# Second-level Winograd sums made by adding DMAs, gated blocks added in the store path, and one more product split twice

## The chip, the cores and the metric

The kernel runs on one core of a Trainium2 chip. The metric is the device time of one execution in microseconds (us). Before the change three runs gave 1852.26, 1853.48 and 1853.75 us, so the median is 1853.48 us.

## What is computed

All in float32, with S = 2048 tokens, D = 1024 and F = 3584:

```python
x = A_x                                              # 1 x 2048 x 1024
g = sigmoid((x * gate_w).sum(-1, keepdims=True))
a = einsum("bsd,ed->bse", x, dft_hid_re)
b = einsum("bsd,ed->bse", x, dft_hid_im)
y = einsum("ts,bse->bte", dft_seq_re, a) - einsum("ts,bse->bte", dft_seq_im, b)
h = einsum("bsd,df->bsf", x, B_w1) + B_b1
h = where(h > 0, h, 0) ** 2
o = einsum("bsf,fd->bsd", h, B_w2) + B_b2
return g * y + (1 - g) * o
```

## The kernel before

Four matrix products do nearly all of the work, one after the other: stage x (the hidden DFT, whose result is called `ab`), stage C (the sequence DFT of `ab`, result `y`, which is multiplied by the gate and kept in DRAM as `gy`), stage h in two parts (`x` times `w1`, then ReLU and square, kept in DRAM as `h`; part 0 has four rows of tiles to a step, part 1 has three), and stage o (`w2` times `h`, then bias, `1 - g`, plus `gy`, then `out`).

Each stage is a Winograd form of Strassen's product: 2 x 2 blocks, seven products in place of eight, in the order 1, 2, 5, 6, 3, 7, 4 (`WIDE`, `TALL_C`, `TALL_O`). Left factors come from sums S1 to S4 of the left blocks, right factors from T1 to T4 of the right blocks (`FACTORS`). A product can be split a second time in the same way ("twice"): seven smaller products in place of eight steps of matmuls, with sums of its own (`SUMS_L2`, `SUMS_R2`). Which products are split twice stands in `TWICE_X`, `TWICE_C`, `TWICE_O`, `TWICE_H`; the numbers in `TWICE_C` and `TWICE_O` say for how many pairs of inner blocks. What isn't split twice runs through `direct`. Stages x and h use `wide`, stages C and o use `tall`.

The data are 128 x 1024 float32 tiles (512 KB). Every factor goes to TensorE as two parts: ScalarE copies the tile to a rounded `hi`, VectorE subtracts to get `lo`, and a tile product is three matmuls, hi*hi, hi*lo and lo*hi (`Operand`, `Group.run`). For 256-column left tiles both parts lie in one tile, `both`. So for each factor there is one pass of ScalarE and one of VectorE; each Winograd sum costs one more pass of VectorE. A finished group of matmuls lies in PSUM (four pools of two banks); ScalarE or VectorE takes it up (`put`, `add`), which frees the banks for a later group. Where a group goes on from an earlier result, ScalarE first copies that to PSUM (`Group.prepare`).

SBUF is cut into 55 slots of one tile (`SLOTS`). Loads are issued by SyncE's queue (SP). Stores, and all DMAs that add into their destination (`accum_op=ADD`), are issued by GpSimd's queue (POOL). Before the change two kinds of adding DMA are in use: with `lands`, a first-level sum of two blocks from DRAM is made by a plain load of one and an adding load of the other into the same slot (`Part.load`); and stage h stores T1 and T3 of `h` for stage o with a store and an adding store into a DRAM block (`Kept.store`, `sums_far`).

The kernel records all its instructions first. `plan` gives each a due time and runs a model of engines, queues and slots; `emit` writes the instructions out in the order that came of it and chains each engine to that order, so every instruction has line L1209 in the profile. Inside a queue nothing overtakes.

The second-level right sums before the change, all with subtraction:

```python
SUMS_R2 = {"T1": ((0, 1), (0, 0), SUB), "T2": ((1, 1), "T1", SUB), "T3": ((1, 1), (0, 1), SUB),
           "T4": ((1, 0), "T2", SUB)}
```

Their blocks are loaded whole into slots of their own, and VectorE makes each sum in a slot of its own. In part 1 of stage h, `TWICE_H[1]` is `(1, 2, 5, 3, 4)`: products 6 and 7 run through `direct`, at 8 steps of 18 matmuls (144) each, and a product split twice takes 7 steps (126). At the end of stage o, `final` multiplies each of the 15 first output blocks by its gate row, loads its `gy` block over SP and adds it with VectorE, then stores; the last block goes by halves (`last`).

Of the kernel before, what the change touches and what calls it, by code (L numbers as in the profile page):

```python
# [19 lines left out]
WIDE, TALL_C, TALL_O = ((1, 2, 5, 6, 3, 7, 4),) * 3  # L20
TWICE_X, TWICE_C, TWICE_O = (1, 2, 5, 3, 4), {1: 1, 2: 4, 3: 4, 4: 4, 5: 2}, {1: 2, 2: 3, 3: 3, 4: 3, 5: 2, 6: 1}
# [24 lines left out]
SUMS_L2 = {"S1": ((1, 0), (1, 1), ADD), "S2": ("S1", (0, 0), SUB), "S3": ((0, 0), (1, 0), SUB),  # L46
           "S4": ((0, 1), "S2", SUB)}
SUMS_R2 = {"T1": ((0, 1), (0, 0), SUB), "T2": ((1, 1), "T1", SUB), "T3": ((1, 1), (0, 1), SUB),
           "T4": ((1, 0), "T2", SUB)}
# [5 lines left out]
def gated_mix_kernel(ctx: ExitStack, tc: tile.TileContext, x4, xn, w4, ct, w1a, w1b, w2, b1, b2, gw, out):  # L55
# [53 lines left out]
    class Op:  # L109


        def __init__(self, engine, name, args, kwargs):
# [6 lines left out]
            if name == "dma_start":  # L119
                self.time, self.load = ISSUE[engine], n * P * 4 / RATE[0]  # L120
                if "accum_op" in kwargs:
                    self.time, self.load = ADDING[0], ADDING[1] * self.load
# [8 lines left out]
            self.after, self.then, self.new, self.latest, self.landed = set(), [], [], None, False  # L131

# [167 lines left out]

    class Operand:
# [107 lines left out]
    steps = []  # L409
# [8 lines left out]
    class Sums:  # L418


        def __init__(self, get, sums, keep=False, far=(), lands=(), shared=None, near=()):
# [30 lines left out]
        def early(self, key):  # L452

            e = self.of(key, near=True)
            self.made[key] = Part(e.far())
# [6 lines left out]
    def seven(order, second, new_u, c11, c12, c21, c22, put, add, direct, twice, slots, sign=1, flip=False):  # L462
# [12 lines left out]
        def six(k, ps):  # L475
            put(u, k, ps)
            add(c12, k, ps, 3 in before[6], c22, sign)
# [6 lines left out]
        for p in order:  # L484
            if p == 1:
                product(1, None, one, False, slots)
            elif p == 2:
                product(2, one, c11, True, slots, 6 in before[2])
            elif p == 3:
                product(3, c12, c12, True, 0, sign=sign)  # L490
# [4 lines left out]
            elif p == 6 and 6 in second:  # L495
                twice(6, one, u, lambda k: add(c12, k, u[k].slot, 3 in before[6], c22, sign), 2 in before[6], 1, -1)
# [11 lines left out]
    def tall(left, right, ksteps, order, second, first, target, final, last=None, lands={}, shared=None):  # L508
# [55 lines left out]
        def twice(p, old, new, ends, drop, sign, less=1):  # L564
# [25 lines left out]
            r2 = {q: Sums(lambda j, c, q=q: right[2 * q + j, c].of(r), SUMS_R2, True) for q in range(k)}  # L590
# [11 lines left out]
            def onward(dst, key, ps):  # L602

                if old:
# [3 lines left out]
                    if less < 0:  # L608
# [19 lines left out]
            def five(_, ps):  # L628
                key = block(1, 1)
                add(new, block(0, 1), ps)  # L630
                if old:
# [7 lines left out]
                    nc.vector.tensor_tensor(flat(at), flat(at), flat(tmp[0, 0].slot), op=ADD)  # L639
# [7 lines left out]
                else:  # L647
                    add({key: new[key]}, key, ps, ends and not more, src={key: new[block(1, 0)]})
# [45 lines left out]
    def wide(left, right, rows, order, second, target, final, sign=1, onto_old=False, flip=False, lands={},  # L694
             shared=None):
# [67 lines left out]
        def twice(p, old, new, ends, drop, sign, less=1):  # L763
# [3 lines left out]
            r2 = Sums(lambda q, c: right[q, c].of(r), SUMS_R2, True)  # L767

            def takes(first, m, c, ends=False):
                def f(rp, ps):  # L770
                    k = m, c, rp
                    if not first:
                        add(new, k, ps, ends, sign=sign)
# [19 lines left out]
            for p2, group in (*(begin if steps else begin[::-1]), (3, other), (6, chain), (2, last), (7, chain),  # L793
# [13 lines left out]
    def x_stage():  # L807
# [7 lines left out]
        def final(dst, ps, sign):  # L815
            if ps is not None:
# [5 lines left out]
             final, -1, True, lands=LAND_X, shared=shared)  # L822
# [3 lines left out]
    h_far = {(j, q, t): Kept(f"h{j}{q}{t}") for j in range(2) for q in range(7) for t in range(4) if j + t // 2}  # L826
    sums_far = {(q, c): {k: Kept(f"{k}{q}{c}", 2) for k in ("T1", "T3")} for q in range(7) for c in range(2)}

    def h_stage(part):
# [3 lines left out]
        def target(i, n, k):  # L833
# [4 lines left out]
            far = [h_far[i, q, 2 * n + c]] if i + n else []  # L838
# [412 lines left out]
```

## Time and profile before

| | |
|---|---|
| median of three runs | 1853.48 us |
| the profiled execution's own time | 1852.4 us |
| span in its trace (first to last instruction) | 1850.6 us |
| matmuls of 128 x 512 | 8034 |
| VectorE instructions | 1746 (16 of them read back an accumulator, and go with an instruction of the program), busy 1753.4 us |
| ScalarE instructions | 1254, busy 1090.8 us |
| DMAs issued by SP and POOL | 628 and 260 |

The profiled execution's time is 1.8 us above its span, and 1.1 us below the median. Times within the trace count from the start of the span. "PE" is TensorE, "PEld" its weight load, "DVE" VectorE, "ACT" ScalarE. A row of the view by stretches shows for each stretch its length, then each engine's busy time with its number of instructions, the granted clock, and the mean busy share of the core's DMA engines. A row of the timeline shows start, duration, engine, operation, and in brackets how long the engine had been idle and what ended that.

### The profile page before, as it was taken

The page shows a single profiled execution, that of the slowest core. Times are in us where ns is not written, and L with a number is a line of the kernel's source. Part 1 is how long each engine was busy: PE and PEld are TensorE (multiplying, and loading weights), DVE is VectorE, ACT ScalarE, POOL GpSimd, SP SyncE. Part 2 cuts the span into 40 slices and gives each one's busy share as a digit, 9 for nine tenths or more (in the row PEclk, how much of TensorE's full clock was granted, in tenths as well). Part 3 has the DMA queues.
Part 4 walks back from the last instruction along what each step waited for, and adds up shares of the span by engine and source line. Part 5 has one row for each costly group of instructions (what it writes and reads, how often), then busy time and mean ns, then how long its engine had stood idle before and what let it go on. Part 6 is the DMA issues. An engine that isn't in the chain of part 4 may idle for free.

```text
span 1850.6 us, 22073 instructions
## 1 busy us (share of the span) xinstructions
PE 1831.6 (99%) x8078; PEld 1511.9 (82%) x8078; DVE 1753.4 (95%) x1746; ACT 1090.8 (59%) x1254; POOL 169.2 (9%) x264
## 2 busy tenths in 40 slices
PE   9999999999999999999999999999999999999998
PEld 7888887888888888888888887888888888888886
DVE  8997999889999999899999999978999999999998
ACT  6474656364453454466583699777976554456352
POOL 0100200001110001000110112202210001100001
PEclk9999999999999999999999999999999999999999
DMA  7762989449998379544563798857994658838935
GB/s 236 261 243 87 377 305 394 167 151 292 294 371 348 136 248 393 210 149 171 165 244 103 243 310 268 264 187 222 310 339 175 216 178 288 301 131 314 362 121 204
DMA packets 131484, 452.37 MB, mean 244 GB/s; under 512 B 14496, under 2 KB 23984, under 8 KB 131376
## 3 DMA queue, kind: packets, MB, share of 16 engines
q1 hardware_dynamic: 94016, 323.15, 48.0%
q0 software_dynamic: 37072, 127.43, 22.5%
q8 instruction: 63, 1.03, 0.2%
q10 hardware_dynamic: 288, 0.39, 0.1%
q14 instruction: 45, 0.37, 0.1%
HBM read 341.85 MB, written 109.06 MB: 244 GB/s over the span
## 4 chain that ended last, share of the span: by engine, by line
PE 82%; DVE 7%; ACT 4%; issue 3%; DMA 3%; POOL 0%; SPq 0%; DVEq 0%; ACTq 0%; POOLq 0%
PE ps L1209 82%; DVE lo L1209 3%; ACT h L1209 2%; DMA raw<-in_x 2%; ACT hi L1209 2%; DVE h L1209 1%; DVE o L1209 1%; DVE sum L1209 1%; DMA raw<-in_ct 0%; DMA h<-h 0%; DVE u L1209 0%; DVE both L1209 0%; ACT ps L1209 0%; DVE raw L1209 0%; POOL h L1209 0%
## 5 line engine op out<-in xcount | busy, mean ns | idle before, releaser
L1209 PE MATMUL ps<-hi 128*128 128x512 f32 x1866 | 727.0, 390 | 8.6 <-ACT hi L1209 3.5
L1209 PE MATMUL ps<-hi,lo 128*128 128x512 f32 x1866 | 725.9, 389 | 0.6 <-DVE lo L1209 0.6
L1209 PE MATMUL ps<-lo,hi 128*128 128x512 f32 x1866 | 725.7, 389 | 0.4 <-DVE lo L1209 0.4
L1209 ACT ACTIVATE hi<-raw 128x1024 fp32r<-128x1024 f32 (+2 forms) x367 | 373.1, 1033 | 252.4 <-DVE raw L1209 119.8
L1209 PE MATMUL ps<-hi,both 128*128 128x512 f32 x1624 | 501.9, 389 | 1.1 <-DVE both L1209 1.1
L1209 DVE TENSOR_TENSOR lo<-raw,hi 128x1024 fp32r<-128x1024 f32 (+2 forms) x367 | 429.7, 1192 | 30.2 <-ACT hi L1209 19.5
L1209 PEld LDWEIGHTS ps<-hi 128*128 128x128 f32 x1866 | 350.6, 188 | 85.1 <-ACT hi L1209 7.3
L1209 PEld LDWEIGHTS ps<-hi,lo 128*128 128x128 f32 x1866 | 350.4, 188 | 74.3 <-DVE lo L1209 1.6
L1209 PEld LDWEIGHTS ps<-lo,hi 128*128 128x128 f32 x1866 | 350.3, 188 | 73.9 <-DVE lo L1209 1.3
L1209 ACT ACTIVATE hi<-sum 128x1024 fp32r<-128x1024 f32 x244 | 249.7, 1036 | 198.3 <-DVE sum L1209 140.2
L1209 PEld LDWEIGHTS ps<-hi,both 128*128 128x128 f32 x1624 | 304.7, 188 | 65.2 <-DVE both L1209 1.9
L1209 PE MATMUL ps<-lo,both 128*128 128x512 f32 x812 | 315.9, 389 | 0.0
L1209 DVE TENSOR_TENSOR lo<-sum,hi 128x1024 fp32r<-128x1024 f32 (+1 forms) x244 | 288.2, 1196 | 12.3 <-PE ps L1209 8.8
L1209 DVE TENSOR_TENSOR raw<-raw 128x1024 f32<-128x1024 f32 (+1 forms) x178 | 211.1, 1205 | 5.6 <-DMA raw<-in_x 1.8
L1209 DVE TENSOR_TENSOR sum<-raw 128x1024 f32<-128x1024 f32 (+2 forms) x180 | 184.3, 1031 | 9.7 <-PE ps L1209 5.8
L1209 PEld LDWEIGHTS ps<-lo,both 128*128 128x128 f32 x812 | 152.4, 188 | 31.6
L1209 DVE TENSOR_TENSOR sum<-raw,sum 128x1024 f32<-128x1024 f32 (+2 forms) x135 | 147.5, 1094 | 3.7 <-PE ps L1209 2.8
L1209 ACT ACTIVATE u<-ps 128x1024 f32<-128x1024 f32 x103 | 99.1, 968 | 84.6 <-PE ps L1209 68.5
L1209 ACT ACTIVATE both<-sum 128x512 fp32r<-128x512 f32 x116 | 70.9, 623 | 72.2 <-DVE sum L1209 57.8
L1209 DVE TENSOR_TENSOR h<-h,ps 128x1024 f32<-128x1024 f32 (+1 forms) x84 | 87.8, 1068 | 2.4 <-ACT u L1209 1.9
L1209 ACT ACTIVATE ps<-u 128x1024 f32<-128x1024 f32 x70 | 67.7, 970 | 25.2 <-DVE u L1209 13.6
L1209 ACT ACTIVATE both<-raw 128x512 fp32r<-128x512 f32 x87 | 53.8, 624 | 46.3 <-DVE raw L1209 21.2
(60 smaller groups left out, 915.5 us busy)
## 6 DMA issues: line engine op xcount, KB each, us to landing
raw<-in_ct SPq DMA_DIRECT2D x133, 512.0 KB, 8.3
raw<-in_w SPq DMA_DIRECT2D x92, 512.0 KB, 5.6
raw<-h SPq DMA_DIRECT2D x78, 512.0 KB, 5.4
raw<-ab SPq DMA_DIRECT2D x72, 512.0 KB, 9.9
raw<-copy SPq DMA_DIRECT2D x62, 512.0 KB, 4.7
raw<-in_x SPq DMA_DIRECT2D x59, 512.0 KB, 6.4
T<-h POOLq DMA_DIRECT2D x48, 512.0 KB, 10.0
copy<-raw POOLq DMA_DIRECT2D x46, 512.0 KB, 6.8
```

What stands on the lines that cost most here:

```text
L1209: made = getattr(real[op.engine], op.name)(*(actual(a) for a in op.args), **{k: actual(v) for k, v in op.kwargs.items()})
```

## The change

Six things change together.

1. The second level's signs are turned so that T1 to T4 are sums (`SUMS_R2` as in the first level; S1 and S4 of `SUMS_L2` and the take-up of product 5 change sign with them).
2. A second-level T1 or T3 whose blocks both come from DRAM can be made in place: the class `Onto` keeps one block's slot and issues an adding load of the other block into it. For that, the base block's own `hi` and `lo` have to be made before. `LAND2_C`, `LAND2_H` and `LAND2_O` say where this is done; stage x is left as it was. Where T1 is made so in `wide`, the second-level products begin with 1 instead of 5.
3. Stage h stores T1 and T3 for 7 of 14 right blocks only (`MADE`), and all blocks of `h`; stage o makes the other T1 and T3 with adding loads (`LAND_O`). In stage C, T3 of the first level no longer lands by an adding load (`LAND_C`).
4. For the first 12 output blocks, `gy` is added by an adding DMA from DRAM (`ADD_O`), ahead of the store on the same queue.
5. Product 6 of part 1 of stage h is split twice.
6. The planner counts adding stores to DRAM as dearer, holds back POOL DMAs due more than 20 us later while SP's or ScalarE's queue moves data, and a DMA held so gets a wait on the VectorE or ScalarE instruction that ended last in its model.

Counted in the two kernels' written-out instructions:

| | before | after |
|---|---|---|
| 128 x 512 matmuls | 8034 | 8016 |
| VectorE instructions: stages x, C, h part 0, h part 1, o | 215, 556, 232, 200, 527 | 215, 538, 220, 219, 510 |
| ScalarE instructions | 1254 | 1244 |
| DMAs by SP | 628 | 604 |
| DMAs by POOL | 260 | 306 |
| of these, adding into a slot | 38 | 108 |
| of these, adding into DRAM | 32 | 16 |

The diff, cut to its core:

```diff
-LAND_X, LAND_C, LAND_H, LAND_O = {"T1": 4, "T3": 2}, {"T1": 16, "T3": 4}, ({"T1": 4}, {"T1": 4, "T3": 4}), {}
+LAND_X, LAND_C, LAND_H, LAND_O = {"T1": 4, "T3": 2}, {"T1": 16}, ({"T1": 4}, {"T1": 4, "T3": 4}), {"T1": 14, "T3": 4}
-TWICE_H = (1, 2, 5, 3, 4, 6), (1, 2, 5, 3, 4)
+ADD_O = range(12)
+LAND2_X, LAND2_C, LAND2_H, LAND2_O = {}, {1: {"T1": 1, "T3": 1}, 2: {"T1": 4, "T3": 4}, 3: {"T1": 4, "T3": 4}, 4: {"T1": 2, "T3": 2}, 5: {"T1": 1, "T3": 1}}, ({1: ("T1", "T3"), 2: ("T1", "T3"), 5: ("T1", "T3"), 3: ("T1", "T3"), 4: ("T1", "T3"), 6: ("T1", "T3")}, {1: ("T3",), 2: ("T3",), 5: ("T1", "T3"), 3: ("T1", "T3"), 4: ("T1", "T3"), 6: ("T3",)}), {2: {"T1": 3, "T3": 3}, 3: {"T1": 2, "T3": 2}, 4: {"T1": 2, "T3": 2}, 5: {"T1": 1, "T3": 1}, 6: {"T1": 1, "T3": 1}}
+MADE = {"T1": 7, "T3": 7}
+TWICE_H = (1, 2, 5, 3, 4, 6), (1, 2, 5, 3, 4, 6)
...
-ADDING = 0.85, 2.1
+ADDING = 0.85, 2.1, 2.65
...
-LATE = 80.0
+LATE, PATIENT = 80.0, (20.0, 0)
...
-SUMS_R2 = {"T1": ((0, 1), (0, 0), SUB), "T2": ((1, 1), "T1", SUB), "T3": ((1, 1), (0, 1), SUB),
-           "T4": ((1, 0), "T2", SUB)}
+SUMS_R2 = {"T1": ((0, 1), (0, 0), ADD), "T2": ((1, 1), "T1", ADD), "T3": ((1, 1), (0, 1), ADD),
+           "T4": ((1, 0), "T2", ADD)}
...
+    class Onto(Near):
+        def __init__(self, base, b):
+            super().__init__("onto")
+            self.blocks, self.b = [base], b
+            base.uses += 1
...
+        def sum(self):
+            base, b = self.blocks[0], self.b
+            self.slot, self.done = base.slot, base.done
+            nc.gpsimd.dma_start(self.slot, b.at if isinstance(b, Kept) else b, accum_op=ADD)
...
                 a, b, op = self.sums[key]
+                other = self.get(*a if a != (1, 1) else b) if key in self.ontos else None
+                if key in self.ontos and not isinstance(other, (Near, View)) and not isinstance(
+                        self.get(*b if a != (1, 1) else a), (Near, View)):
+                    self.made[key] = Onto(self.of(b if a != (1, 1) else a), other)
+                    return self.made[key]
...
-            for p2, group in (*(begin if steps else begin[::-1]), (3, other), (6, chain), (2, last), (7, chain),
+            for p2, group in (*(begin if steps and "T1" not in r2.ontos else begin[::-1]), (3, other), (6, chain), (2, last), (7, chain),
                               (4, chain)):
...
-    h_far = {(j, q, t): Kept(f"h{j}{q}{t}") for j in range(2) for q in range(7) for t in range(4) if j + t // 2}
-    sums_far = {(q, c): {k: Kept(f"{k}{q}{c}", 2) for k in ("T1", "T3")} for q in range(7) for c in range(2)}
+    h_far = {(j, q, t): Kept(f"h{j}{q}{t}") for j in range(2) for q in range(7) for t in range(4)}
+    sums_far = {(q, c): {k: Kept(f"{k}{q}{c}", 2) for k in spread(MADE, 2 * q + c, 14)} for q in range(7)
+                for c in range(2)}
...
-            ready(add, cycle((nc.sync,)))
+            lands = len(made_o) in ADD_O
+            made_o.append(dst)
+            if not lands:
+                ready(add, cycle((nc.sync,)))
...
-            nc.vector.tensor_tensor(flat(dst.slot), flat(dst.slot), flat(add.slot), op=ADD)
+            if lands:
+                nc.gpsimd.dma_start(dst.slot, gy[i, n, c, rp].at, accum_op=ADD)
+            else:
+                nc.vector.tensor_tensor(flat(dst.slot), flat(dst.slot), flat(add.slot), op=ADD)
+                add.used()
...
+                    if (e == "gpsimd" and op.due - t > PATIENT[0] and len(free) >= PATIENT[1]
+                            and any(q in moving or rings[q] for q in ("sync", "scalar"))):
+                        op.held = True
+                        continue
+                    if op.held:
+                        op.gate = done[-1]
...
+        if op.gate:
+            tc.add_manual_dep(made.ins, op.gate.made, mybir.DependencyInfo(
+                mybir.DependencyClass.Sync, mybir.DependencyReason.DATA), reason="held")
```

More of the change, by code (lines that the diff above doesn't have):

```diff
@@ L121, in __init__ @@
                 if "accum_op" in kwargs:
-                    self.time, self.load = ADDING[0], ADDING[1] * self.load
+                    far = outs[0].base.home == "fixed"
+                    self.time, self.load = ADDING[0], ADDING[2 if far else 1] * self.load
             elif engine == "tensor":
@@ L454, in early @@
             e = self.of(key, near=True)
-            self.made[key] = Part(e.far())
+            self.made[key] = e.far()
             return e
@@ L476, in six, with five @@
             put(u, k, ps)
-            add(c12, k, ps, 3 in before[6], c22, sign)
+            if 5 in before[6]:
+                add(c12, k, ps, 3 in before[6], c22, sign)
+        def five(k, ps):
+            put(c22, k, ps)
+            add(c12, k, ps, True)
         def seven(k, ps):
@@ L488, in seven @@
                 product(2, one, c11, True, slots, 6 in before[2])
+            elif p == 3 and 5 in before[3]:
+                product(3, c12, c12, True, 0, sign=sign)
             elif p == 3:
-                product(3, c12, c12, True, 0, sign=sign)
+                assert 6 in before[3] and sign == 1
+                product(3, u, c12, False, slots)
+            elif p == 5 and 3 in before[5] and 5 in second:
+                twice(5, None, c22, lambda k: add(c12, k, c22[k].slot, True), False, 1)
+            elif p == 5 and 3 in before[5]:
+                direct(5, None, slots, five, [c22, c12], 1)
             elif p == 4 and 7 in before[4]:
@@ L495, in seven @@
             elif p == 6 and 6 in second:
-                twice(6, one, u, lambda k: add(c12, k, u[k].slot, 3 in before[6], c22, sign), 2 in before[6], 1, -1)
+                twice(6, one, u, (lambda k: add(c12, k, u[k].slot, False, c22, sign)) if 5 in before[6] else False,
+                      2 in before[6], 1, -1)
             elif p == 7 and 7 in second:
@@ L629, in five @@
                 key = block(1, 1)
-                add(new, block(0, 1), ps)
+                add(new, block(0, 1), ps, less=1 if old else -1)
                 if old:
@@ L647, in five @@
                 else:
-                    add({key: new[key]}, key, ps, ends and not more, src={key: new[block(1, 0)]})
+                    add({key: new[key]}, key, ps, ends and not more, src={key: new[block(1, 0)]}, less=-1)
             fresh = old is not new
@@ L772, in f @@
                     if not first:
-                        add(new, k, ps, ends, sign=sign)
+                        add(new, k, ps, ends, sign=-sign if c else sign)
                     elif old:
@@ L1134, in finish @@
         op.landed = True
+        if op.engine in ("vector", "scalar") and not op.load:
+            done[:] = [op]
         for sight in op.ins + op.outs:
```

58 lines of the change are left out of this document (38 added, 20 removed).

## The prediction

> **What bounds the kernel now.** I read the page's head first, for the busy shares, and its chain of waits.
>
> ```profile
> span 1850.6 us, 22073 instructions
> ...
> PE 1831.6 (99%) x8078; PEld 1511.9 (82%) x8078; DVE 1753.4 (95%) x1746; ACT 1090.8 (59%) x1254; POOL 169.2 (9%) x264
> ...
> PE 82%; DVE 7%; ACT 4%; issue 3%; DMA 3%; POOL 0%; SPq 0%; DVEq 0%; ACTq 0%; POOLq 0%
> ```
>
> TensorE is busy all the time, VectorE nearly so. So time is won here only by fewer matmuls or fewer stalls of TensorE, and VectorE is the engine most likely to cause stalls. To count these I took the first and the last matmul from the timeline, and the view by stretches, with one stretch for each of x, C, h part 0, h part 1 and o.
>
> ```profile
> 6.43 0.73 PE L1209 MATMUL ps<-hi 128*128 128x512 f32 x2 [0.93 <-ACT hi L1209]
> ...
> 1843.06 0.39 PE L1209 MATMUL ps<-hi,lo 128*128 128x512 f32 x1
> ```
>
> ```profile
> 0.00:288.90 288.90, 284.31 (x1268) 234.82 (x1269) 262.91 (x242) 166.95 (x172) 30.84 (x57) 0.99 0.72 257
> 288.90:859.00 570.10, 569.06 (x2509) 470.65 (x2509) 535.25 (x552) 291.19 (x332) 33.56 (x50) 1.00 0.72 254
> 859.00:1134.30 275.30, 272.57 (x1201) 225.04 (x1200) 269.75 (x238) 194.17 (x221) 35.20 (x55) 1.00 0.66 214
> 1134.30:1346.50 212.20, 209.81 (x919) 171.85 (x919) 192.32 (x201) 172.16 (x224) 44.57 (x64) 1.00 0.82 253
> 1346.50:1850.60 504.10, 495.84 (x2185) 409.57 (x2183) 493.17 (x517) 266.33 (x309) 25.02 (x39) 1.00 0.67 239
> ```
>
> Part 1 of stage h, cut at its seven products (order 1, 2, 5, 6, 3, 7, 4):
>
> ```profile
> 1134.30:1163.80 29.50, 28.82 (x127) 23.54 (x127) 29.19 (x30) 27.19 (x35) 6.84 (x9) 1.00 1.05 311
> 1163.80:1192.70 28.90, 28.85 (x128) 23.58 (x127) 28.82 (x31) 18.88 (x24) 6.57 (x9) 1.00 0.87 249
> 1192.70:1221.80 29.10, 28.86 (x127) 23.59 (x127) 29.10 (x31) 26.96 (x36) 5.89 (x11) 1.00 0.94 336
> 1221.80:1254.40 32.60, 32.60 (x145) 27.00 (x145) 17.73 (x19) 19.16 (x24) 0.00 (x0) 1.00 0.15 56
> 1254.40:1283.30 28.90, 28.85 (x128) 23.59 (x127) 28.67 (x31) 19.02 (x24) 4.83 (x5) 1.00 0.82 210
> 1283.30:1315.90 32.60, 32.60 (x146) 26.99 (x145) 28.37 (x31) 32.32 (x44) 10.90 (x15) 1.00 1.04 314
> 1315.90:1346.50 30.60, 29.23 (x128) 23.58 (x127) 30.44 (x34) 28.64 (x41) 9.54 (x15) 1.00 0.95 312
> ```
>
> Product 6 (fourth row) runs its 144 matmuls in 32.6 us without a stall, which gives a pace of 0.2267 us. Against that pace the stages lose: x 288.9 - 6.4 - 1224 x 0.2267 = 5.0 us; C 570.1 - 2508 x 0.2267 = 1.5; h part 0 275.3 - 1200 x 0.2267 = 3.3; h part 1 212.2 - 918 x 0.2267 = 4.1; o, up to its last matmul, 496.8 - 2184 x 0.2267 = 1.7. That is 15.6 us of stalls in the whole kernel, beside 6.4 us ahead of the first matmul and 7.6 behind the last. The larger stalls outside stage x, from the timeline of TensorE:
>
> ```profile
> 308.78 0.50 PE L1209 MATMUL ps<-lo,hi 128*128 128x512 f32 x1 [0.41 <-DVE lo L1209]
> 309.91 0.50 PE L1209 MATMUL ps<-hi,lo 128*128 128x512 f32 x1 [0.63 <-DVE lo L1209]
> ...
> 1128.77 0.47 PE L1209 MATMUL ps<-hi 128*128 128x512 f32 x1 [2.31 <-DVE h L1209]
> ...
> 1669.48 0.74 PE L1209 MATMUL ps<-hi,both 128*128 128x512 f32 x2 [1.10 <-DVE both L1209]
> ```
>
> All four are ended by VectorE, and in part 1 of h VectorE is full in every product split twice (28.82 of 28.9 us) and idle for 14.9 us in product 6. So VectorE's work, stage by stage, is what to follow.
>
> **The change part by part.**
>
> Matmuls first. Product 6 of h part 1 falls from 144 to 126 matmuls; nothing else on TensorE changes in number: 18 x 0.2267 = 4.1 us less. But the five products there that are split twice lose, against 126 x 0.2267 = 28.56 us, 0.9, 0.3, 0.5, 0.3 and 2.0 us, and the two direct ones nothing. I charge product 6 their mean, **+0.8** (0.3 to 2.0).
>
> VectorE's work, at the durations by form:
>
> ```profile
> L1209 DVE TENSOR_TENSOR sum<-raw 128x1024 f32<-128x1024 f32 x112 | 135.4, 1218 | 6.0 <-DMA raw<-in_x 3.5 <-PE ps L1209 2.2 <-DMA raw<-copy 0.3
> L1209 DVE TENSOR_TENSOR lo<-raw,hi 128x768 fp32r<-128x768 f32 x23 | 21.9, 951 | 4.0 <-ACT hi L1209 3.8
> L1209 DVE TENSOR_TENSOR h<-h,ps 128x512 f32<-128x512 f32 x23 | 15.5, 681 | 0.0
> ```
>
> C loses 18 passes of 1024 elements (21.9 us), h part 0 loses 12 (14.6 us), and o loses 17, the 12 additions of `gy` among them (20.7 us). Part 1 of h gains 19: 5 of 1024, 7 of 768, 7 of 512, together 6.1 + 6.7 + 4.8 = 17.5 us. x is as it was, and keeps its 5.0 us of stalls.
>
> In C the stalls at 308.8 and 309.9 (1.5 us together) stand at the end of a chain of VectorE work in the first product. There two sums, 2.4 us of VectorE, go away. I take **-1.2** (0 to -1.5), since the start of the stage is also full of gate sums that stay. In o the stall at 1669.5 (1.3 us against the pace) lies in product 3, which loses four sums, 4.9 us; **-0.9** (0 to -1.3).
>
> The two parts of h must be taken together, since work for part 1 is done in part 0 where slots allow. VectorE had 269.75 + 192.32 = 462.1 us of work in 487.5 us, so 25.4 idle; it will have 462.1 - 14.6 + 17.5 = 465.0 in 487.5 - 4.1 = 483.4, so 18.4 idle. That is less, but most of what is used up is the gap in product 6, for which nobody waited. In part 1 alone it is tight: 192.3 + 17.5 = 209.8 us of work against 900 x 0.2267 = 204.0 us of matmuls. If nothing is carried ahead, and VectorE runs at the 99% of the rows above, the part lasts 209.8 / 0.99 = 211.9 us, 7.9 over its matmuls, of which the old 4.1 and the 0.8 above are counted already: at worst +3.0. At best the 14.6 us taken from part 0 end its stalls, -3.3. Nearest is the first row of part 0, where VectorE had 98% and lost 3.3, as it does now: I take **+0.5**.
>
> The adding loads cost TensorE nothing as long as they land in time. 70 more are issued. Their chain is issue, landing, `hi`, `lo`:
>
> ```profile
> L1209 POOL DMA_DIRECT2D raw<-in_ct x20 | 17.5, 874 | 283.9 <-PE ps L1209 197.6 <-DMA raw<-in_ct 30.8 <-DVE raw L1209 18.1
> ...
> raw<-in_ct POOLq DMA_DIRECT2D x20, 512.0 KB, 9.5
> ...
> L1209 ACT ACTIVATE hi<-raw 128x1024 fp32r<-128x1024 f32 x339 | 352.8, 1054 | 245.1 <-DVE raw L1209 117.8 <-PE ps L1209 79.8 <-DVE lo L1209 13.1
> ```
>
> That is 0.87 + 9.5 + 1.05 + 1.22 = 12.6 us, or 56 matmuls. I counted, in the order in which the changed kernel writes out its instructions, the matmuls between each adding load and the first one that needs it: the closest have 75, 79, 89 and 92, the middle one some 142 (before: from 94 up). So 75 x 0.2267 = 17.0 us cover 12.6, and I cost them at nothing. What they cost when that cover is gone is the rival on the slow side. The base block's own `hi` and `lo` now come ahead of the add; these passes are not new, only earlier, and the smaller distances show it. The 12 additions of `gy` delay only their stores; behind these on POOL stand other stores and adding loads, and the last four blocks still go the old way, so the 7.6 us behind the last matmul stay. The 88 DMAs that were held get a wait each; at least 149 matmuls (34 us) stand between any of them and the first matmul that needs it, so a wait of some us on POOL is covered too.
>
> Do the DMA engines bear it?
>
> ```profile
> q1 hardware_dynamic: 94016, 323.15, 48.0%
> q0 software_dynamic: 37072, 127.43, 22.5%
> ...
> DMA to landing us min/median/max: 2.9/9.4/22.6
> ```
>
> SP's queue: 48.0% of 1850.6 us for 617 tiles of 512 KB, 1.44 us each. POOL's: 416 us; its 190 plain DMAs at 1.44 take 274, which leaves 2.0 us for each of the 70 that add. After: 24 fewer by SP (-35), 70 more adding loads (+142), 16 fewer adding stores (-32), 8 fewer plain stores (-12): +63 us, from 70.5% to 74% of the span. Nothing in the sum.
>
> Sum: -4.1 + 0.8 - 1.2 - 0.9 + 0.5 = **-4.9 us**. The span would be 1845.7 and the profiled execution's time 1847.5; taken from the median, 1853.48 - 4.9 = **1848.6 us**.
>
> **The rivals.**
>
> First, VectorE becomes the bound of h part 1 and what it is spared in C and o does not reach TensorE: -4.1 + 0.8 + 3.0 = -0.3, **1853.2 us**. For it: the full rows of part 1. Against it: part 0 is relieved just ahead, and each stall quoted ends on VectorE.
>
> Second, part 0's stalls go as well: its 14.6 us less stand against 3.3 us of stalls, the largest of which (1128.77) ends on VectorE. -4.9 - 0.5 - 3.3 = -8.7, **1844.8 us**. Against it: that stall comes when part 1's own work, which grows, is already being done.
>
> Third, on the other side, **adding loads land late**. Place: the shortest distances, where base block, add, `hi`, `lo` and matmul follow on each other. It decides from a landing of 17.0 - 0.87 - 1.05 - 1.22 = 13.9 us on. At 18 us the chain is 21.1 us, and the four closest loads are short by 4.1, 3.2, 0.9 and 0.3: +8.5, **1857.1 us**. For it: adding stores of `T` in h took up to 22.6 us (the last row above), with DMA shares of 0.82 to 1.05 around them. Against it: those wrote to DRAM, half of them go, and the median was 9.4.
> The Trainium skill (DMA: Bandwidth & Descriptors, section "Issuing engines are not separate DMA queues") says that transfers from all queues run on the same 16 engines and interleave there. By that rule POOL's added traffic delays SP's loads too, which speaks for this rival; the trace agrees as far as the DMA share of 1.05 and the long landings fall together in part 1, but there the traffic shrinks.
>
> **How the numbers follow.** Chances: the forecast 0.49, the first rival 0.19, the second 0.16, the third 0.16. From no change a measurement here tells about 0.2%, or 3.7 us: faster means below 1849.8, slower above 1857.2. The second rival is faster wholly; the forecast's own range, from its terms' bounds without the second rival's gain, is -4.1 + 0.3 - 1.5 - 1.3 = -6.6 to -4.1 + 2.0 + 3.0 = +0.9, so 1846.9 to 1854.4, most of it below 1849.8 (0.46 of 0.49). The first rival counts as the same nearly always (0.17), the third as slower for 0.14. Faster 0.62, same 0.22, slower 0.16. The range, 1844.8 to 1857.0, reaches the second and almost the third rival.
>
> **What would show it.** Right: 8016 matmuls at 0.2267 us; the stalls at the start of C and in product 3 of o gone or below 0.5 us; h part 1 at 204.0 us plus 4 to 6; VectorE busy 513, 255, 210 and 472 us in C, h part 0, h part 1 and o; adding loads at a median of 8 to 11 us; some 7.6 us behind the last matmul. Wrong: stalls of TensorE that end on `ACT hi` behind a DMA that adds (third rival); h part 1 above 212 us with VectorE full throughout (first); a longer tail, if stores that wait for `gy` pile up at the end.

## The result, and the profile after

| | before | after |
|---|---|---|
| median of 8 runs each | 1853.07 us | 1847.76 us (1846.31 to 1849.36) |
| ratio | 1 | 0.997, 95% interval 0.996 to 0.9981 |
| span of the profiled execution | 1850.6 us | 1845.7 us |

The change saves 5.3 us, or 0.3%, and the interval leaves out 1; 4.9 us and a time of 1848.6 us were forecast. The page's head of the changed kernel:

```profile
span 1845.7 us, 22089 instructions
...
PE 1827.6 (99%) x8060; PEld 1508.2 (82%) x8060; DVE 1718.6 (93%) x1718; ACT 1082.8 (59%) x1244; POOL 211.8 (11%) x310
```

Its stages, cut where the first matmul of x, C, h part 0, h part 1 and o stands (length; busy time of TensorE, its weight loads, VectorE, ScalarE, POOL; clock; DMA share; GB/s):

```profile
0.00:288.70 288.70, 283.71 (x1268) 234.71 (x1269) 263.02 (x243) 165.62 (x172) 28.75 (x52) 0.99 0.73 254
288.70:857.20 568.50, 568.50 (x2510) 470.78 (x2509) 519.04 (x536) 293.68 (x333) 53.64 (x76) 1.00 0.81 272
857.20:1131.20 274.00, 273.04 (x1202) 224.88 (x1201) 260.36 (x230) 196.82 (x224) 38.81 (x58) 1.00 0.69 212
1131.20:1343.90 212.70, 207.19 (x902) 168.11 (x901) 202.96 (x215) 161.16 (x211) 39.82 (x57) 1.00 0.80 235
1343.90:1845.70 501.80, 495.19 (x2185) 409.76 (x2183) 473.26 (x498) 265.53 (x309) 50.73 (x68) 1.00 0.78 258
```

The first matmul starts at 6.44 us and the last at 1838.70. Taking the matmuls of each stage at 0.2267 us off its length, as in the prediction, leaves its stalls:

| stalls of TensorE, us | x | C | h part 0 | h part 1 | o | behind the last matmul's start |
|---|---|---|---|---|---|---|
| before | 5.0 | 1.5 | 3.3 | 4.1 | 1.7 | 7.6 |
| after | 4.8 | 0.0 | 2.0 | 8.7 | 0.0 | 7.0 |

So C and o lost all their stalls, part 0 of h some, and part 1 of h got twice as many: with 18 matmuls fewer it takes 212.7 us, half a microsecond more than before. The seven products of part 1, in their order 1, 2, 5, 6, 3, 7, 4:

```profile
1131.20:1162.20 31.00, 29.11 (x127) 23.49 (x126) 27.02 (x28) 26.14 (x34) 6.85 (x9) 1.00 1.02 299
1162.20:1191.10 28.90, 28.90 (x128) 23.62 (x127) 25.77 (x27) 17.69 (x24) 3.81 (x5) 1.00 0.69 173
1191.10:1221.50 30.40, 29.06 (x127) 23.45 (x126) 29.46 (x32) 26.59 (x35) 6.23 (x11) 1.00 0.72 257
1221.50:1250.80 29.30, 28.87 (x127) 23.59 (x127) 28.61 (x31) 10.54 (x13) 1.56 (x2) 1.00 0.49 132
1250.80:1281.10 30.30, 29.16 (x128) 23.54 (x127) 30.09 (x34) 19.53 (x24) 6.57 (x8) 1.00 0.81 204
1281.10:1313.70 32.60, 32.60 (x146) 26.99 (x144) 32.11 (x35) 32.34 (x44) 7.40 (x12) 1.00 0.91 271
1313.70:1343.90 30.20, 29.48 (x128) 23.43 (x127) 29.90 (x34) 28.32 (x42) 7.40 (x13) 1.00 0.91 303
```

Against 28.56 us for a product split twice, product 1 now loses 2.4 us (before 0.9), 5 loses 1.8 (0.5), 3 loses 1.7 (0.3), and product 6, the new one, 0.7. VectorE has time to spare in product 1 (27.0 of 31.0 us), so its load is not what stalls TensorE there. In products 5, 6, 3 and 4 it is busy for 97 to 99%, so there its load stays a suspect. The experiments look for the causes.

The DMAs: shares of the queues of SP and POOL, then POOL's landing times for tiles of `raw` (its 46 plain stores of copies among them), then two rows of adding loads with their medians:

```profile
q1 hardware_dynamic: 90560, 310.57, 45.5%
q0 software_dynamic: 43824, 153.12, 31.3%
...
DMA to landing us min/median/max: 2.9/7.1/15.8
```

```profile
raw<-in_ct POOLq DMA_DIRECT2D x34, 512.0 KB, 8.5
...
raw<-h POOLq DMA_DIRECT2D x19, 512.0 KB, 7.9
```

In the median the adding loads land no later than before (9.5 us for `in_ct` then). Two of `in_ct` took 15.8 and 14.6 us, both in stage C, which has no stall.

### The profile page after: what moved, and what is told of

It reads as the page before. It is cut to its first block, busy times and chain, and to the rows that moved or that the text cites. A ratio compares the mean times of both kernels' runs of the same rounds, so it can differ in the third digit from the quotient of the medians.

```text
span 1845.7 us, 22089 instructions
## 1 busy us (share of the span) xinstructions
PE 1827.6 (99%) x8060; PEld 1508.2 (82%) x8060; DVE 1718.6 (93%) x1718; ACT 1082.8 (59%) x1244; POOL 211.8 (11%) x310
## 3 DMA queue, kind: packets, MB, share of 16 engines
q1 hardware_dynamic: 90560, 310.57, 45.5%
q0 software_dynamic: 43824, 153.12, 31.3%
## 4 chain that ended last, share of the span: by engine, by line
PE 84%; DVE 7%; ACT 5%; DMA 2%; issue 2%; SPq 0%; DVEq 0%; ACTq 0%
PE ps L1281 84%; DVE h L1281 2%; DVE lo L1281 2%; ACT hi L1281 2%; ACT h L1281 2%; DMA raw<-in_x 2%; DVE sum L1281 1%; ACT u L1281 1%; DVE u L1281 1%; ACT ps L1281 1%; DMA raw<-in_w1b 0%; DVE raw L1281 0%; DVE o L1281 0%; SPq L1281 0%; DVE both L1281 0%
## 5 line engine op out<-in xcount | busy, mean ns | idle before, releaser
L1281 ACT ACTIVATE hi<-raw 128x1024 fp32r<-128x1024 f32 (+2 forms) x418 | 424.8, 1036 | 290.7 <-PE ps L1281 107.7
L1281 DVE TENSOR_TENSOR lo<-raw,hi 128x1024 fp32r<-128x1024 f32 (+2 forms) x418 | 491.2, 1195 | 26.2 <-ACT hi L1281 19.2
L1281 ACT ACTIVATE hi<-sum 128x1024 fp32r<-128x1024 f32 (+1 forms) x199 | 201.8, 1028 | 162.0 <-DVE sum L1281 102.6
L1281 DVE TENSOR_TENSOR lo<-sum,hi 128x1024 fp32r<-128x1024 f32 (+1 forms) x199 | 233.5, 1185 | 20.5 <-PE ps L1281 12.3
L1281 DVE TENSOR_TENSOR raw<-raw 128x1024 f32<-128x1024 f32 (+1 forms) x187 | 222.0, 1206 | 15.0 <-DMA raw<-copy 7.6
L1281 DVE TENSOR_TENSOR sum<-raw 128x1024 f32<-128x1024 f32 (+2 forms) x156 | 154.8, 998 | 17.6 <-PE ps L1281 14.4
L1281 ACT ACTIVATE u<-ps 128x1024 f32<-128x1024 f32 x95 | 92.6, 980 | 51.9 <-PE ps L1281 38.2
L1281 DVE TENSOR_TENSOR sum<-raw,sum 128x1024 f32<-128x1024 f32 (+2 forms) x113 | 120.5, 1066 | 2.6 <-PE ps L1281 2.0
L1281 DVE TENSOR_TENSOR both<-sum,both 128x512 fp32r<-128x512 f32 x116 | 78.5, 684 | 6.6 <-ACT both L1281 6.5
L1281 DVE TENSOR_TENSOR h<-h,ps 128x1024 f32<-128x1024 f32 (+1 forms) x76 | 81.2, 1079 | 0.5
```

Of the source, the lines that this page charges most:

```text
L1281: made = getattr(real[op.engine], op.name)(*(actual(a) for a in op.args), **{k: actual(v) for k, v in op.kwargs.items()})
```

## The experiments

The theories. **A**: the prediction's account; the split saves 4.1 us less 0.8, and the sums moved to DMAs save some 2 us in C and o. **B**: part 1 of h is bound by VectorE, the split gives back what it saves, and the gain is VectorE's relief alone. **C**: part of the gain hangs on how POOL's DMAs are kept out of SP's way. Two came up on the way. **D**: in the new order of second-level products, two steps that use the same PSUM banks follow each other too closely. **E**: loads that land late hold up ScalarE, and with it the take-ups that stand behind them in its order.

The runs were timed in three sets, each beside the kernel before (medians 1853.17 us for e1 to e4, 1852.73 for e5 to e8, 1853.88 for e9 to e12), and the change in a set of its own (1853.07). So a difference between two medians of the table can be off by a microsecond for the sets alone, and the ratios decide. Also, all but e8 and e9 were planned anew, so that a small edit moves other instructions too: e5 leaves stage x alone, and x has 3.9 us of stalls there against 4.8. Stage figures are stalls in the profiled execution, found as above.

| run | median us | ratio to before (95%) | stalls in C, h 0, h 1, o |
|---|---|---|---|
| the change | 1847.76 | 0.997 (0.996 to 0.9981) | 0.0, 2.0, 8.7, 0.0 |
| e1 without the split | 1851.55 | 0.9998 (0.9989 to 1.0007) | 0.0, 2.0, 9.4, 0.0 |
| e2 the split alone | 1864.51 | 1.0068 (1.0055 to 1.0081) | 1.6, 4.2, 17.4, 3.5 |
| e3 no second-level adds | 1854.74 | 1.0009 (1.0 to 1.0018) | 1.2, 0.7, 12.8, 3.0 |
| e4 no `gy` adds | 1849.18 | 0.998 (0.9972 to 0.9989) | 0.0, 2.0, 8.6, 1.2 |
| e5 order 5, 1, 3 in part 1 | 1846.97 | 0.9966 (0.9954 to 0.9979) | 0.0, 3.2, 7.8, 0.0 |
| e6 no held DMAs | 1858.69 | 1.0035 (1.0023 to 1.0047) | 0.0, 2.8, 9.9, 6.6 |
| e7 all T stored | 1865.54 | 1.0069 (1.0056 to 1.0081) | 0.0, 2.3, 21.7, 7.1 |
| e8 adds in halves | 1848.74 | 0.998 (0.997 to 0.9989) | 0.0, 2.1, 9.5, 0.0 |
| e9 no adding stores of T | 1845.45 | 0.9958 (0.9946 to 0.9971) | 0.0, 2.0, 6.4, 0.0 |
| e10 held DMAs alone | 1856.28 | 1.0016 (1.0007 to 1.0025) | 1.2, 1.2, 8.5, 4.2 |
| e11 order 5, 1, 3 in both parts | 1847.36 | 0.9969 (0.9958 to 0.9981) | 0.0, 1.2, 9.0, 0.0 |
| e12 the same, T1 stored for 6 | 1843.66 | 0.9949 (0.9937 to 0.9962) | 0.0, 1.7, 5.0, 0.0 |

### Is the split worth anything? (e1, e2)

```diff
 e1, in the changed kernel
-TWICE_H = (1, 2, 5, 3, 4, 6), (1, 2, 5, 3, 4, 6)
+TWICE_H = (1, 2, 5, 3, 4, 6), (1, 2, 5, 3, 4)
 e2, in the kernel before
-TWICE_H = (1, 2, 5, 3, 4, 6), (1, 2, 5, 3, 4)
+TWICE_H = (1, 2, 5, 3, 4, 6), (1, 2, 5, 3, 4, 6)
```

> The changed kernel with product 6 of h part 1 run through direct again (18 matmuls more, 27 VectorE instructions fewer in that part). Theory A, the prediction's own account: the split is worth 4.1 us of matmuls less 0.8 us of stalls, so this run is 3.3 us slower than the changed kernel, near 1851 us. Theory B: part 1 is bound by VectorE, so the split gives back in stalls what it saves in matmuls, and the whole gain comes from the VectorE work that adding DMAs took over: within 1.5 us of 1847.8 us, with part 1 of h again near 212 us.

> The kernel before with nothing changed but the split of product 6 (18 matmuls fewer, 28 VectorE instructions more in h part 1, no sum moved to an adding DMA). Theory A: 3.3 us faster than before, near 1849.8 us. Theory B: VectorE must do some 26 us more in a part that had 20 us of VectorE idle against 4 us fewer matmuls: part 1 lasts (192 + 26) / 0.99 = 220 us instead of 212 if nothing is carried ahead, so up to 8 us slower than before, 1856 to 1861 us.

Part 1 of h in e1, then in e2, then its product 3 in e2:

```profile
1131.20:1348.70 217.50, 211.07 (x919) 171.53 (x918) 180.44 (x190) 170.13 (x222) 39.47 (x56) 1.00 0.79 231
```

```profile
1135.50:1356.90 221.40, 212.26 (x902) 170.13 (x902) 215.61 (x226) 161.82 (x208) 42.38 (x62) 0.98 0.80 242
...
1252.30:1291.30 39.00, 33.48 (x127) 24.16 (x126) 38.86 (x43) 22.17 (x28) 7.39 (x8) 0.96 0.66 161
```

Each theory is right in one of the two. In the changed kernel the split is worth 3.8 us by the medians (4.8 us in part 1: 217.5 against 212.7), as A said. Alone it costs 11 us, in B's direction and beyond B's 1856 to 1861 us: VectorE gets 215.6 us of work, fills product 3 (38.86 of 39.0 us), and TensorE stalls there for 10 us. The parts do not add up: the split alone is +11.3 us, all the rest without it -1.6 us (not told apart from nothing by its interval), both together -5.3.
But e1 also shows what B can't: with VectorE busy for only 180.4 of 217.5 us, part 1 still stalls for 9.4 us, against 4.1 before the change. Of these, 2.7 us lie in product 1 and 1.5 in product 5, where VectorE has work for 27.2 of 31.3 and 25.3 of 30.1 us, so they don't come from how much it has to do. In products 3 and 4 it is busy for 98% and 94%, and there e1 can't tell.

### Which adds pay? (e3, e4)

```diff
 e3
-LAND2_X, LAND2_C, LAND2_H, LAND2_O = {}, {1: {"T1": 1, "T3": 1}, 2: {"T1": 4, "T3": 4},
...
+LAND2_X, LAND2_C, LAND2_H, LAND2_O = {}, {}, ({}, {}), {}
 e4
-ADD_O = range(12)
+ADD_O = range(0)
```

> The changed kernel with all second-level T1 and T3 made by VectorE again (no in-slot adding loads at that level; the split, the gy adds, the halved T stores and the planner's rule for held DMAs stay). VectorE gets 22, 12, 9 and 10 instructions more in C, h part 0, h part 1 and o. Theory A: the stalls at the start of C and in o come back in part and h stays, 2 to 3 us over the changed kernel, near 1850.3 us. Theory B: the split goes unpaid in h, so over 6 us more than the changed kernel, 1854 us or above, most of it in the two parts of h.

> The changed kernel with gy loaded over SP and added by VectorE for all 16 blocks, as before (12 VectorE instructions more in o, 12 adding DMAs fewer). Stage o had 1.7 us of stalls before and none after; product 3 of o loses its four sums still. Theory A: o's term was 0.9 us, so 0.5 to 1.7 us over the changed kernel, 1848.3 to 1849.5 us. Theory B puts the gain in VectorE relief everywhere: 1.5 us or more, 1849.3 us or above.

Part 1 of h in e3:

```profile
1132.20:1349.00 216.80, 208.65 (x902) 167.94 (x901) 214.71 (x226) 163.23 (x210) 34.69 (x51) 1.00 0.72 220
```

The second-level adds are worth 7.0 us, against A's 2 to 3: without them VectorE is full again in part 1 (214.7 of 216.8 us) and product 3 alone loses 7.8 us. The size is B's, the place is not: the two parts of h together lose 2.8 us, C and o 4.2. The `gy` adds are worth 1.4 us by the medians, inside A's bounds, but the two intervals overlap; what the traces show is that o stalls for 1.2 us when VectorE makes these sums, and not at all otherwise.

### Do late or many adding DMAs cost anything? (e8, e6, e10, e7)

```diff
 e8, in emit, for each adding DMA into a slot
+            made = real[op.engine].dma_start(args[0][:, 0:1, :], args[1][:, 0:1, :], **op.kwargs)
...
+            args = [a[:, 1:2, :] for a in args]
...
 e6
-LATE, PATIENT = 80.0, (20.0, 0)
+LATE, PATIENT = 80.0, (1e9, 0)
 e7
-..., LAND_O = ..., {"T1": 14, "T3": 4}
+..., LAND_O = ..., {}
...
-MADE = {"T1": 7, "T3": 7}
+MADE = {"T1": 14, "T3": 14}
```

e10 is the kernel before with point 6 of the change and nothing else.

> The changed kernel in the same order, but each of the 108 adding DMAs into a slot issued as two halves of 256 KB: POOL's issue time for them doubles (+0.87 us each), and each lands later by about that. The prediction's cover: the closest adding loads have 17.0 us against a chain of 12.6 us, so 13.5 us still fit and the time stays within 1.0 us of 1847.8 us. The prediction's third rival (adding loads that land late): stalls of TensorE on hi behind adding loads, 3 us or more slower, 1851 us or above.

> The changed kernel without the planner's rule for held POOL DMAs (and so without the waits that the rule adds); all else is as changed. Theory A/B: the gain is matmuls and VectorE's relief, DMAs have cover: within 1.0 us of 1847.8 us. Theory C: adding loads and stores on POOL collide with SP's loads unless they are held back, so that part of the gain hangs on the rule: 3 us or more slower, 1851 us or above.

> The kernel before with the planner's part of the change alone (held POOL DMAs with their waits, dearer adding stores, stores due 30 us ahead of the end); no sum moved, no split. Theory C, strong form: the rule is worth several us by itself, 1850 us or below. Theory F: it is worth something only where POOL carries many adding loads; with 38 of them the queue's holding back does nothing or delays stores into busier stretches: 1852 us or above.

> The changed kernel with T1 and T3 of h stored by stage h for all 14 right blocks, as before (16 adding stores and 16 first stores more in h, 14 of the adding loads of o fewer). VectorE's instructions stay the same in h and fall by 5 in o. Theory A/B: within 1.0 us of 1847.8 us. Theory C: POOL's queue and the DMA engines are what is full in the two parts of h (DMA shares of 0.7 to 1.0 there), so the halving of these stores carries part of the gain: 3 us or more slower, 1851 us or above, with the loss in h or at the start of o.

In e8 the adds land about 1 us later (median from the first issue to the last landing 9.0 us against 8.0). The time moves by 1.0 us by the medians, and the intervals overlap; most of it is in part 1 of h (0.8). C and o, with 69 of the 108 adds, stay without a stall. So the cover that the prediction counted is there, as far as 1 us more of landing tests it. But e6 and e7 came out far on C's side, 11 and 18 us slower than the change. In e6 most is lost in o; from the chain of waits there, and part 1 of h in e7 with its product 2 and a row of ScalarE's timeline in it:

```profile
1801.44 12.17 DMA raw<-in_w
```

```profile
1131.60:1357.30 225.70, 212.43 (x901) 171.31 (x900) 205.15 (x217) 163.07 (x211) 48.75 (x68) 0.98 0.84 240
1162.30:1197.10 34.80, 31.95 (x128) 25.63 (x127) 24.01 (x25) 19.40 (x25) 8.45 (x11) 0.90 0.94 254
...
1174.61 1.06 ACT L1281 ACTIVATE hi<-raw 128x1024 fp32r<-128x1024 f32 x1 [8.30 <-DMA raw<-copy]
```

In both, a load stands in the way: in e6 the chain goes through a load of `w2` for 12.2 us, while four `gy` adds run, in e7 ScalarE waits 8.3 us at one `hi` for a load of a copy, at a DMA share of 0.94. That load was issued at 1166.56 and took 8.0 us, so it came late in the main because it was issued late. VectorE has 10 us to spare in that product of e7 (24.0 of 34.8). That TensorE's stalls there come from this wait is argued from their order in time; no run tests it.
For e6 the cause stays open. The changed kernel has the same `w2` load at the same DMA share of 1.0, and there it takes just as long (13.4 us from issue to landing, 13.8 in e6), ScalarE waits 1.2 us for it (1.7 in e6), and o has no stall. What differs is that the four adds start 28 matmuls earlier there, ahead of the load by 8.9 us against 4.8. And the first longer stall of o in e6, at 1807.4, ends on VectorE's `lo` and comes 7.8 us before the load has landed. So C holds in that the rule is worth 11 us beside the many adds; how it does it is not shown. The rule for held DMAs is no gain in itself: alone, in e10, it costs 0.16%, as theory F had it. There too part 1 of h stalls for 8.5 us, and each of these stalls ends on VectorE.

### What stalls part 1 of h? (e5, e9)

ScalarE's `hi` of full-size tiles in part 1, before and after, with what ended its idle time:

```profile
L1209 ACT ACTIVATE hi<-raw 128x1024 fp32r<-128x1024 f32 x22 | 23.1, 1050 | 5.0 <-PE ps L1209 3.5 <-DVE lo L1209 1.2 <-DMA raw<-in_x 0.4
```

```profile
L1281 ACT ACTIVATE hi<-raw 128x1024 fp32r<-128x1024 f32 x29 | 30.4, 1052 | 30.6 <-DMA raw<-copy 22.2 <-PE ps L1281 5.7 <-DMA raw<-in_x 2.6
```

ScalarE waits 24.8 us for loads where it waited 0.4. The kernel chains ScalarE to one order, so a `hi` that waits for a load holds up the take-ups of PSUM behind it. These are six waits: three of them, 12.6 us, are for SP's loads, and three, 12.2 us, for adding loads of POOL. The first one of the part and the longest one:

```profile
1144.80 1.06 ACT L1281 ACTIVATE hi<-raw 128x1024 fp32r<-128x1024 f32 x1 [2.61 <-DMA raw<-in_x]
1262.06 1.06 ACT L1281 ACTIVATE hi<-raw 128x1024 fp32r<-128x1024 f32 x1 [7.89 <-DMA raw<-copy]
```

The longest is for an adding load, issued at 1253.65 and landed 8.3 us later. A wait alone doesn't stall TensorE: in stage C ScalarE waits 8.4 us for one load, at 329.39, and C has no stall. In product 1, though, the chain of waits and TensorE's timeline lead from a late load to the stalls:

```profile
1132.27 12.45 DMA raw<-in_x
```

```profile
1148.50 0.50 PE L1281 MATMUL ps<-hi 128*128 128x512 f32 x1 [0.83 <-ACT ps L1281]
1158.01 0.50 PE L1281 MATMUL ps<-hi 128*128 128x512 f32 x1 [1.06 <-DVE u L1281]
```

That is theory **E**. In products 5, 3 and 4 there is another kind of stall, at the start of the third step:

```profile
1199.88 0.50 PE L1281 MATMUL ps<-hi 128*128 128x512 f32 x1 [0.50 <-ACT h L1281]
1259.41 0.47 PE L1281 MATMUL ps<-hi 128*128 128x512 f32 x1 [0.27 <-DVE h L1281]
1322.79 0.50 PE L1281 MATMUL ps<-hi 128*128 128x512 f32 x1 [0.32 <-DVE h L1281]
```

Products 5, 3 and 4 are those with T1 made in the slot, so they begin with 1, 5, 3, and steps 5 and 3 share their banks: theory **D**. A third kind stands late in products 5, 6, 3 and 4; the two largest:

```profile
1217.33 0.50 PE L1281 MATMUL ps<-hi 128*128 128x512 f32 x1 [0.83 <-DVE h L1281]
1276.87 0.47 PE L1281 MATMUL ps<-hi 128*128 128x512 f32 x1 [0.86 <-DVE h L1281]
```

In these four products VectorE is busy for 97 to 99%, and the four stalls end on it. They come to 3.4 of the part's 8.7 us, and fit theory **B**.

In e5, `EARLY` names the numbers of rows for which the old order comes back; part 1 has three rows, part 0 four.

```diff
 e5
+EARLY = (3,)
...
-            for p2, group in (*(begin if steps and "T1" not in r2.ontos else begin[::-1]), (3, other), ...
+            order2 = (*(begin if steps and ("T1" not in r2.ontos or rows in EARLY) else begin[::-1]), (3, other), ...
+            made2 = {}
+            for p2 in (1, 5, 3, 6, 2, 7, 4) if "T1" in r2.ontos else [p for p, _ in order2]:
+                made2[p2] = l2.operand(l_, rows * P), r2.operand(r_)
...
+            for p2, group in order2:
+                step(*made2[p2], group)
...
+        if isinstance(o, Onto) and o.first is not None:
+            ready(o.first, engines)
 e9, in emit
+        if "accum_op" in op.kwargs and op.outs[0].base.home == "fixed":
+            continue
```

> The changed kernel, with one thing undone in part 1 of h: where T1 is made in the slot, the second-level products begin with 5, 1, 3 again in place of 1, 5, 3 (the factor of product 1 is still made first, so that T1 can be added onto its slot). Theory D: in the order 1, 5, 3 steps 5 and 3 follow each other in the same PSUM banks, and with three rows only 6 matmuls (1.36 us) lie between the end of the first bank's sum and the next matmul into it, less than a take-up takes (1.0 to 1.2 us and the signalling); that makes the stalls some 8.5 us into products 5, 3 and 4 of part 1, 0.77 + 0.44 + 0.59 = 1.8 us. They vanish here: near 1846.0 us. Theory B: VectorE's load is what delays the take-ups, and their order changes nothing: 1847.3 to 1848.3 us.

> The changed kernel in the same order, but the 16 adding stores that complete T1 and T3 of h in DRAM are left out (so the part of stage o that uses these sums computes with half of them). Theory E: in part 1 of h the stalls come from SP loads that land late while the DMA engines are full (share 1.02 in product 1, a load of x4 took 12.4 us) and stand at the head of ScalarE's queue, ahead of take-ups that TensorE waits for. With about 3 us of DMA time less for each adding store, product 1's stall of 2.5 us falls below 1.5 us and part 1 loses 1.5 us or more of its 8.7 us of stalls: 1846.3 us or below. Theory B (VectorE's load alone): part 1 keeps 8 to 9 us of stalls and the time stays at 1847.3 us or above.

In e5 all three stalls at the third step are gone: TensorE's matmuls go on there at 0.23 us (1200.10, 1200.33, 1200.56). Product 3 loses 0.4 us instead of 1.7 and product 5 1.2 instead of 1.8. D holds as to the cause, but the new schedule gives it all back in product 1 (3.3 us) and in part 0 (+1.2): the two parts of h stall for 11.0 us together, against 10.7. The total, 0.8 us better, is not told apart from the changed kernel by the intervals, and in the trace it lies in stage x. In e9, product 1 and part 1 of h:

```profile
1131.40:1160.20 28.80, 28.80 (x127) 23.57 (x126) 27.24 (x28) 25.94 (x34) 5.85 (x7) 1.00 0.79 233
1131.40:1341.80 210.40, 206.80 (x901) 168.13 (x900) 203.15 (x215) 160.96 (x210) 34.26 (x50) 1.00 0.73 220
```

With VectorE's work the same (203.2 us), the load that ScalarE waited for takes 6.6 us instead of 12.5, product 1's stall falls from 2.4 to 0.2 us, and the DMA share there from 1.02 to 0.79. Products 5, 3 and 4 keep theirs, and ScalarE still waits 7.8 us at its longest `hi`: only for the wait in product 1 is a stall shown that goes with it. This wait and the stalls of product 1 go together in other runs too: 2.6 and 2.5 us in e8, 2.8 and 2.7 in e1 and e4, 3.2 and 3.3 in e5. E holds for product 1, and B is out for it. The total of e9 is not told apart from the changed kernel by the intervals.

### A better version (e11, e12)

```diff
 e11, on top of e5
-EARLY = (3,)
+EARLY = (3, 4)
-... 4: ("T1", "T3"), 6: ("T3",)}), ...
+... 4: ("T1", "T3"), 6: ("T1", "T3")}), ...
 e12, on top of e11
-MADE = {"T1": 7, "T3": 7}
+MADE = {"T1": 6, "T3": 7}
```

> The changed kernel with second-level products in the order 5, 1, 3 in both parts of h, and T1 of product 6 in part 1 made by an adding load too. Theory D: the stall at the third step of the products of part 0 (0.3 us at 944.4 in the changed kernel) and the three of part 1 go, and one more VectorE sum goes in product 6: 1 to 2 us faster than the changed kernel, 1846 us or below. Otherwise 1847 us or above.

> The kernel of e11 with T1 of h stored for 6 right blocks in place of 7, which takes one store and one adding store from part h and adds one adding load in o. Theory E: less DMA work in part 1 of h, so at most as long as e11 there: 1846 us or below, h part 1 shorter by 0 to 1 us than in e11. If o's VectorE or its loads are what matters, 1847 us or above.

Part 1 of h in e11, then in e12 with its product 1 ahead:

```profile
1130.30:1343.30 213.00, 206.32 (x901) 168.23 (x900) 203.00 (x214) 162.10 (x211) 41.69 (x59) 1.00 0.81 236
```

```profile
1130.20:1159.70 29.50, 28.88 (x128) 23.57 (x127) 29.25 (x30) 27.67 (x36) 8.56 (x10) 1.00 1.02 274
1130.20:1339.20 209.00, 206.12 (x901) 168.40 (x900) 203.14 (x214) 162.64 (x211) 41.90 (x59) 1.00 0.82 235
```

e11 missed: part 0 gains 0.8 us, but product 1 of part 1 loses 4.4. e12 is the best of all, 1843.66 us: 0.51% faster than before, and by the medians 4.1 us faster than the change (the two intervals just touch, 0.9962 and 0.996; all five runs of e12 are faster than the fastest of the change). Its part 1 keeps 5.0 us of stalls, with product 1 down to 0.9 at the same DMA share of 1.02. There the `in_x` load takes 10.5 us, and ScalarE doesn't wait for it. So the share alone does not decide; what counts is which transfer is late and what stands behind it.
e12's part 1 is 4.0 us shorter than e11's, where 0 to 1 was expected of one store and one adding store less. Most of that is product 1. How much of this is the store and how much another order of the plan, no run tells.

## Why the prediction was right, and where its terms were off

- **Matmuls, -4.1**: 8016 were run, at the same pace. e1 puts the whole split, in the changed kernel, at -3.8 us by the medians; forecast were -4.1 + 0.8 = -3.3. Product 6 stalls for 0.7 us, against 0.8. So A's price holds, but only with VectorE relieved: alone the split costs 11 us.
- **C, -1.2, and o, -0.9**: both stages lost all their stalls, -1.5 and -1.7 us. The cause was named rightly: e4 brings 1.2 us of o's stalls back with 12 VectorE sums, e3 1.2 in C.
- **The two parts of h, +0.5 beside the 0.8**: mis-sized. Part 0 gained 1.3 us and part 1 lost 4.6, so +3.3 where +1.3 stood. Part 1 lasts 212.7 us, above the 204.0 plus 4 to 6 that was named as a sign, and above the first rival's 212; but VectorE isn't full throughout, as that rival needs. The failing step is that these stalls were weighed by VectorE's work alone. Two others were shown: take-ups behind a `hi` that waits for a late load, 2.4 us in product 1 (e9), and two steps in the same banks after each other, 1.8 us in products 5, 3 and 4 (e5). The other 4.5 us of part 1's 8.7 end on VectorE for the most part and weren't taken apart. The change of order was in the diff and was not costed.
- **VectorE's work**: -34.8 us in all against -39.7 forecast; part 1 has 203.0 us, not 209.8. In part 1 the reason is mainly that work was carried ahead: its row has 14 instructions more than before where 19 were added, and part 0 has 260.4 us where 255 stood. Besides, consecutive passes overlap at their ends (in the trace of before one that starts at 1126.54 and takes 0.96 us is followed by the next at 1127.41), so a mean duration per pass overstates what each adds or takes away; C lost 16.2 us where 21.9 stood.
- **The adding loads at nothing**: right as to TensorE in C and o. Their median landing is 8.5 and 7.9 us against the 13.9 from which they would cost, and e8 bears out 1 us of the cover. (The view counts a landing from the start of the issue, so the chain holds the 0.87 us of issue twice; it is 11.8 us.) No stall of TensorE behind the start ends on `ACT hi`, which was the sign of the third rival. But three of ScalarE's six long waits in part 1 are for adding loads, 12.2 us where there was none; what they cost, no run takes apart. The load that was shown to cost time, in product 1, is a plain one on SP's queue. The rule that was named beside that rival, of the Trainium skill (DMA: Bandwidth & Descriptors, "Issuing engines are not separate DMA queues"), agrees with e9, where leaving out POOL's adding stores shortens an SP load that ScalarE waits for from 12.5 to 6.6 us.
- **The DMA share**: 74% were forecast, 45.5 + 31.3 = 76.8% measured. The cost of an adding DMA, 2.0 us, came out too low. With the changed kernel's POOL queue (31.3% of 1845.7 = 578 us for 182 plain and 124 adding DMAs) beside that of before (416 us for 190 and 70) the two equations give 3.1 us for an adding one and 1.0 for a plain one, if each kind costs the same in both kernels. Pairs of runs that differ by adds give less: 2.9 us for each of the 53 that e3 leaves out (POOL's queue 426 us), 2.3 for each of the 12 of e4 (551 us), 2.1 for each of the 16 of e9 (544 us; four of these are half a tile). And e10, with the DMAs of before, has 426 us where that had 416, so a planned order alone is worth 10 us.
- **Held DMAs and halved T stores at nothing**: wrong as to what they are worth; e6 and e7 lose 11 and 18 us without them. They did not show in the sum because the change brings them along with the adds beside which they pay.
- **The tail**: 0.6 us shorter, forecast unchanged.

The total came out by luck as far as its terms go: the 2.0 us that h cost over its forecast are made up by C, o, x and the tail, which together gave 1.9 us more than theirs, and x and the tail were forecast to stay as they were. What was right without luck is the source of the gain: 18 matmuls fewer, and C and o without stalls.

## What to carry to other kernels

Where two engines are both nearly full, fewer matmuls and moved sums are not worth their own prices: the split alone cost 11 us and with VectorE relieved it saved 4, so price such a pair together, stage by stage. Ahead of a move to DMAs, look at what stands behind each load in the consumer's order: an operand copy that waits for its load also holds up the take-ups of PSUM behind it, even where the DMA engines' mean share over the stage (0.80 in part 1) leaves room. It costs time only where TensorE soon needs one of these take-ups: a wait of 8.4 us in C cost none. When the order of steps changes, count the matmuls between the end of one sum and the next matmul into the same banks.

## What the runs showed of the hardware

An adding DMA of 512 KB took 2.3 to 3.1 us of the DMA engines' time, by the pairs of runs worked out above, where SP's plain loads took 1.42 (45.5% of 1845.7 us for 310.57 MB, or 592 tiles). This is an estimate: the figure hangs on the pair.

Short stalls can cost twice. In product 2 of part 1 in e7 the mean granted clock was 0.90:

```profile
1184.94 0.50 PE L1281 MATMUL ps<-hi 128*128 128x512 f32 x1 [2.09 <-ACT hi L1281]
1186.20 0.80 PE L1281 MATMUL ps<-lo,hi 128*128 128x512 f32 x1 [0.76 <-DVE lo L1281]
```

After these two stalls, of 2.3 and 1.0 us against the pace, a dozen matmuls ran at 0.427 us instead of 0.227. Other stalls left the clock at 1.00: a single one of 2.5 us before the change (at 1128.77), a single one of 2.7 in e11 (at 1159.00), and in e7 itself two of 0.9 and 1.7 us close together (at 1219.14 and 1221.09). What makes the difference, these runs don't show.
